# Attention and a spectral filter on one core: chunk order, later values, filter products on GpSimd

## The chip, the cores and the metric

The kernel runs on one core of one Trainium2 chip. The core has five engines with a queue of instructions each: TensorE (PE in the profile), VectorE (DVE), ScalarE (ACT), GpSimd (POOL) and SyncE (SP, which issues most DMAs). Matmul results go to PSUM, which has eight banks of 128 partitions by 512 float32 values; the other operands lie in SBUF. The metric is the time of one execution in microseconds, as the median of several runs.

## The reference

Two branches are mixed by a gate g per row. S is 2048, D is 448, there are 16 heads of 28, and all inputs are bfloat16. Branch b uses the same x as branch a.

```python
def reference(A_x, A_wqkv, A_wo, B_x, B_w_r, B_w_i, gate_w):
    def _A_ref(x, wqkv, wo):
        ...
        qkv = (lambda x, *d: x.transpose(*d))((x @ wqkv).reshape(B, S, 3, H, Dh), 2, 0, 3, 1, 4)
        ...
        scores = jnp.einsum("bhqd,bhkd->bhqk", q, k) * scale
        p = _softmax(scores, axis=-1)
        o = jnp.einsum("bhqk,bhkd->bhqd", p, v)
        return (lambda x, *d: x.transpose(*d))(o, 0, 2, 1, 3).reshape(B, S, D) @ wo
    def _B_ref(x, w_r, w_i):
        X = (lambda x, axes=(-2,-1): jnp.fft.rfft2(x.astype(jnp.float32), axes=axes))(x, axes=(-2, -1))
        W = w_r + 1j * w_i
        X = X * W
        y = (lambda x, s, axes=(-2,-1): jnp.fft.irfft2(x, s=s, axes=axes).astype(jnp.bfloat16))(X, (S, D), axes=(-2, -1))
        return y
    x = A_x
    g = _sigmoid((x * gate_w).sum(-1, keepdims=True))
    a = _A_ref(x, A_wqkv, A_wo)
    b = _B_ref(x, B_w_r, B_w_i)
    return g * a + (1 - g) * b
```

## The kernel before

**Attention.** The 16 heads form four groups G of four. A chunk is one group with 512 queries (j from 0 to 3), so there are 16 chunks; before, they run in the order ci = 4 G + j. A chunk has 16 packs, one for each 128 keys (kt), and a pack has four units, one per head: a score matmul with 32 rows of contraction into one PSUM bank, the exponential, and a product with the values that adds into the bank psV. Keys and queries of a group lie in KT[G % 2] and QT[G % 2], so those of group G can be projected when group G - 2 has no scores left.

**Two ways to the exponential.** A pack of kind A goes through ScalarE: two score tiles of two banks each (psA, psB) and one activation per tile into the ring P of 20 slots (L862; the first packs into VS). A pack of kind D goes through VectorE: its four scores go to single banks psX, an add and a maximum turn each into the bits of a bfloat16 (L891), and three shifted copies are made of the whole pack (L897); all four sets are multiplied with the values and add up, which stands for the exponential. Which pack is of which kind is settled when the program is built.

**The other work.** It is cut into units that borrow a psX bank: the transposes of x, the projections of K, Q (L1116) and values (v, L1276), the first transform of the filter (f1), then for each of 16 slices g: f2, f3, the product with the complex filter W, and i1; then i2 for 16 t's, and the 16 output tiles (L1474). In a slice, f3 leaves its result in PSUM, VectorE multiplies it twice (by the real and by the imaginary part, L1384), GpSimd adds and subtracts (L1391), and i1 on PE reads the sums. After each chunk VectorE copies psV to osb (L1449), the row sums go through DRAM (rs, rgd, RB: four, one and four DMAs on SP), and GpSimd multiplies osb by RB (L1458) into ON. An output tile is one matmul group with the filter's result Z and three with ON (groups 0 to 2), and then one with ON of group 3. The last chunk is normalised by transposes on VectorE (L1468 to L1472). Output tiles leave through four slots of ost, and a slot is free when its store has landed.

**What sets the order.** A planner (class Plan) runs when the program is built. It walks through the work with a duration per operation, gives each engine its next operation by priority, due time and free banks, and writes out one fixed order per engine; nothing is rearranged on the chip. Units have a point (at, in chunks of progress) from which they may start, and a due point. Operations of VectorE and GpSimd that are marked port are not laid on top of each other in the plan. When PE's load over a window is below z_hard, a group of matmuls with zero weights is put in. Score tiles in this text are counted in PE's order: there are 400 of them, one for each activation of L862.

Of the kernel before, what the change touches and what calls it, by code (L numbers as in the profile page):

```python
# [20 lines left out]
C = 112  # L21
# [6 lines left out]
BITS_MIN = 256.0  # L28

# [128 lines left out]
class Plan:  # L158
# [3 lines left out]
    def __init__(self, cfg):  # L162
        self.cfg = cfg
        self.out = []
# [108 lines left out]
    def run(self):  # L273
# [18 lines left out]
        limit = 1200.0  # L292
        while self.npend > 0 or not self.stream_over():
            eng = min(self.T, key=self.T.get)
            t = self.T[eng]
            if t > limit:
# [113 lines left out]
    def next_tile(self):  # L410
# [7 lines left out]
        while len(units) < size:  # L418
            if cur is None:
# [31 lines left out]
        self.tile = dict(k=k, units=units, ready=ready, slots=slots, grp=k % len(self.sizes))  # L451
        self.ntile += 1
        return self.tile

# [38 lines left out]
    def exp_run(self, e, t):  # L493
# [11 lines left out]
        for p, h in e["units"]:  # L505
            a = self.act_pack[p]
            a["exps"].append(o)
            if len(a["exps"]) == 4:
                ci, kt = divmod(p, 16)
                x = Op("PE", 0, None, [self.v_ready[ci // 4][kt]] + a["exps"], name="pv")  # L510
# [47 lines left out]
    def d_run(self, d, h, bank, t, conc):  # L558
# [19 lines left out]
        self.s_mark(d["p"] // 64, o.end)  # L578
# [3 lines left out]
    def d_sums(self, d):  # L582
        p = d["p"]
        ci, kt = divmod(p, 16)
        vr = self.v_ready[ci // 4][kt]
# [34 lines left out]
    def pe_step(self, t):  # L620
# [35 lines left out]
        pool = c["xbanks"] if (self.started or self.reserve) and any(self.s_left) else self.allb  # L656
# [67 lines left out]
    def s_run(self, tl, t):  # L724
# [13 lines left out]
        for p, h in tl["units"]:  # L738
            G = p // 64
# [5 lines left out]
        fb = self.free_banks(t, self.cfg["xbanks"])  # L745
# [82 lines left out]
    tiles=(2, 2), xbanks=("X0", "X1", "X2"), nring=20, nvar=10, nearly=5, l_pe=0.09, l_act=0.03, pe_lat=0.20,  # L828
    dma_issue=0.6, m_pe=0.2, m_bank=0.1, tol=0.15, max_ahead=9, nd_max=99, d_open=3, ahead=3, d_chunks=1,
    dve_op1=0.605, dve_shift=0.60, pool_shift=2.0, pool_shifts=(), pool_every=0, prio_op1=3, prio_shift=3, sh_max=4, d_urg=0,  # L830
    window=3.413, z_hard=3250, z_soft=3500,
    w_pv=1.0, w_open=0.5, w_new=1.6, w_late=0.5, w_d=3, w_due=2, hungry=1.4, v_rush=0.5, x_rush=4.0, k_rush=5.0, q_rush=0.0, w_hungry=1, sw_pen=0, pv_min=1, ring_urg=2, d_first=True,
# [3 lines left out]
class Emit:  # L836
# [5 lines left out]
    def score(self, p, h, bank):  # L842
        k = self.k
        ci, kt = divmod(p, 16)
        G, j = divmod(ci, 4)
# [27 lines left out]
    def value(self, p, h, rhs, x):  # L873
        k = self.k
        ci, kt = divmod(p, 16)
        G = ci // 4
# [27 lines left out]
class Kernel:  # L904
# [27 lines left out]
    def tiles(self, ctx):  # L932
# [9 lines left out]
        self.psX = [ps.tile([128, 512], F32, name=f"psX{i}") for i in range(len(CFG["xbanks"]))]  # L942
# [37 lines left out]
        self.Wo = sb("Wo", [128, NG, D])  # L980
# [4 lines left out]
        self.t12 = [[sb(f"t{n}{i}", [128, 2 * FP]) for n in (1, 2)] for i in range(2)]  # L985
        self.P = sb("P", [128, CFG["nring"], 512])
# [25 lines left out]
    def plan(self):  # L1012
# [5 lines left out]
        for i, b in enumerate(CFG["xbanks"]):  # L1018
            pl.banks[b] = self.psX[i][:, :]
# [40 lines left out]
    def loads(self):  # L1060
# [10 lines left out]
        self.d_wv = self.dma(self.Wv[0:C, :, 0:D], w3[:, :, 2 * D:3 * D], 9.4, **fast)  # L1071
        self.d_gw = self.dma(self.Wv[0:C, :, D:D + 1], self.gw.rearrange("(c k o) -> k c o", c=NC, o=1), 9.4)
# [21 lines left out]
        self.m_wo = pl.op("POOL", 1.9, lambda e: nc.gpsimd.memset(self.Wo[:, :, :], 0.0), prio=6, port=True)  # L1094
        self.d_wo = []
        wov = self.wo.rearrange("(g h d) n -> h d g n", g=NG, h=4)
        for h in range(4):
            self.d_wo.append(self.dma(self.Wo[32 * h + 1:32 * h + 29, :, :], wov[h], 3.0, [self.m_wo, self.d_bi], prio=7))
# [31 lines left out]
    def square(self, eng, src, i, deps, prio=4, alt=None):  # L1130
# [9 lines left out]
    def head(self):  # L1140
        pl, nc = self.pl, self.nc
        self.o_xT = [[] for _ in range(4)]
        for b in range(4):
            for cp in range(2):
                u = pl.unit(-10, "xT", due=-1, rush=6.0 if b == 0 else CFG["x_rush"])
# [24 lines left out]
        u = pl.unit(-8, "w", due=-1, rush=6.0)  # L1170
# [10 lines left out]
        self.m_wo.deps.append(self.o_wt)  # L1181
        self.queries(0, -6.9945, None, [1, 2, 3], "DVE", deps=[self.o_wt])

    def first(self, which, b, name, sel, one):
# [3 lines left out]
        u = self.proj((-9.5 if b == 0 else -9.0) + 0.1 * b, which, 0, b, name, due=-1, rush=6.0 if b == 0 else CFG["k_rush"])  # L1188
# [13 lines left out]
    def queries(self, G, at, nk, blocks, eng, deps=(), alt=None, span=0.0):  # L1202
# [3 lines left out]
        due = at + 1.5 if G else 0.3  # L1206
# [38 lines left out]
    def group(self, G, at, span=0.18):  # L1245
# [3 lines left out]
        for b in range(4):  # L1249
            u = self.proj(at + span * b, 0, G, b, "k", deps=free, due=at + 1.2)  # L1250
            self.k_ready[G][b] = self.ev_k(u, G, b, deps=free)
            sqs.append(self.square("POOL", self.KT[G % 2][:, 512 * b:512 * b + 512], b, [self.k_ready[G][b], self.sq_use[b]]))
        u = pl.unit(at + span * 4, "kn", due=at + 1.3)
# [12 lines left out]
        u = pl.unit(at + span * 4, "kb", due=at + 1.3)  # L1266
        u.mm(lambda bank: self.mm(bank[:, 0:1], self.mrow4[:, :, :].rearrange("p b h -> p (b h)"), self.one[0:1, 1:2], True, True), n=60, kind="row", deps=[b2])
        nk = u.use("DVE", 0.1, lambda bank, e: nc.vector.tensor_copy(out=self.nks[G % 2][:, :], in_=bank[:, 0:1]), prio=2)
        self.queries(G, at + span * 5, nk, [0, 1, 2, 3], "POOL", deps=free, span=span)


    def values(self):
        nc = self.nc
        self.o_g, evs = [], []
        for t in range(NT):
# [6 lines left out]
            def ev(bank, e, t=t):  # L1282
                out = self.Vb[:, t, :, 1:29]
                in_ = bank[:, 0:448].rearrange("p (h d) -> p h d", d=DH)
                nc.scalar.copy(out=out, in_=in_) if e == "ACT" else nc.vector.tensor_copy(out=out, in_=in_)
            o = u.use("DVE", dict(DVE=0.54, ACT=0.5), ev, deps=[self.m_v1], alt="ACT", prio=2)
            evs.append(o)
            for G in range(1, NG):
                self.v_ready[G][t] = o
            self.o_g.append(u.use("DVE", 0.09, lambda bank, e, t=t: nc.vector.tensor_copy(out=self.glog[:, t:t + 1], in_=bank[:, 448:449]), prio=2))  # L1290
        for b in range(4):
# [4 lines left out]
            o = self.pl.op("DVE", dict(DVE=0.54, POOL=1.0), weigh, evs[4 * b:4 * b + 4] + [self.o_wt], prio=0, port=True)  # L1296
            for t in range(4 * b, 4 * b + 4):
                self.v_ready[0][t] = o

    def gate(self):  # L1300
        pl, nc = self.pl, self.nc
        a = pl.op("ACT", 0.12, lambda e: nc.scalar.activation(out=self.ge[:, :], in_=self.glog[:, :], func=ACT.Exp, scale=-1.0), self.o_g)
        a = pl.op("DVE", 0.1, lambda e: nc.vector.tensor_scalar_add(out=self.ge[:, :], in0=self.ge[:, :], scalar1=1.0), [a], port=True)
        a = pl.op("DVE", 0.25, lambda e: nc.vector.reciprocal(out=self.ge[:, :], in_=self.ge[:, :]), [a])
# [239 lines left out]
```

## Time and profile before

The median of three runs is 417.62 us (414.58 to 419.14). The profiled execution took 417.98 us, of which the span from the first to the last instruction is 416.2 us; its granted TensorE clock is 0.992.

| engine | work in the span | instructions |
|---|---|---|
| PE | matmuls, 394.5 us busy | 5030 |
| DVE | bits, shifts, evictions, 367.7 us | 677 |
| ACT | exponentials above all, 382.4 us | 418 |
| POOL | squares, sums, normalising products, 102.4 us | 144 |

The page divides the span into 40 slices and gives the busy share of each engine in tenths. A line of the groups gives the source line, the engine and operation, output and inputs with shapes, the count, the busy time, the mean duration of one, and the idle time of the engine just before them with what ended it. Durations of instructions that overlap add up to more than the engine's busy time, so the interval from start to start is taken from the timeline. The line number of a matmul is that of a helper (L913), so matmuls are told apart by their tiles.

### The profile page before, as it was taken

The page shows a single profiled execution, that of the slowest core. Times are in us where ns is not written, and L with a number is a line of the kernel's source. Part 1 is how long each engine was busy: PE and PEld are TensorE (multiplying, and loading weights), DVE is VectorE, ACT ScalarE, POOL GpSimd, SP SyncE. Part 2 cuts the span into 40 slices and gives each one's busy share as a digit, 9 for nine tenths or more (in the row PEclk, how much of TensorE's full clock was granted, in tenths as well). Part 3 has the DMA queues.
Part 4 walks back from the last instruction along what each step waited for, and adds up shares of the span by engine and source line. Part 5 has one row for each costly group of instructions (what it writes and reads, how often), then busy time and mean ns, then how long its engine had stood idle before and what let it go on. Part 6 is the DMA issues. An engine that isn't in the chain of part 4 may idle for free.

```text
span 416.2 us, 12278 instructions
## 1 busy us (share of the span) xinstructions
PE 394.5 (95%) x5030; PEld 136.2 (33%) x5030; DVE 367.7 (88%) x677; ACT 382.4 (92%) x418; POOL 102.4 (25%) x144
## 2 busy tenths in 40 slices
PE   7999999999999999999999999999999999999993
PEld 4433343222333323323333223223333322223251
DVE  3547699999999999989999899899998999999991
ACT  3895989999999999999999999999999989999941
POOL 0251102652221323331302242251367111010100
PEclk9999999999999999999999999999999989999998
DMA  8520001221022202021121201100100100010203
GB/s 263 151 62 7 4 2 17 53 41 39 11 57 52 84 8 63 4 64 32 37 74 46 58 8 59 39 28 4 28 3 2 28 2 27 4 50 4 70 8 106
DMA packets 23929, 17.66 MB, mean 42 GB/s; under 512 B 15268, under 2 KB 19281, under 8 KB 23873
## 3 DMA queue, kind: packets, MB, share of 16 engines
q1 hardware_dynamic: 22800, 16.59, 14.8%
q8 instruction: 39, 0.64, 0.7%
q10 hardware_dynamic: 1072, 0.29, 0.3%
q14 instruction: 18, 0.14, 0.1%
HBM read 14.71 MB, written 1.97 MB: 40 GB/s over the span
## 4 chain that ended last, share of the span: by engine, by line
PE 42%; ACT 25%; DVE 16%; issue 6%; DMA 6%; SPq 2%; ACTq 0%; DVEq 0%; POOL 0%
ACT P L862 25%; PE psX L913 15%; PE psV L913 13%; PE psB L913 7%; PE psA L913 7%; DVE VS L897 5%; DVE VS L891 5%; DMA rs<-osb 3%; DMA Qf<-in_A_wqkv_dram 2%; SPq L1055 2%; DMA out_dram<-ost 2%; DVE osb L1449 1%; DVE t L1384 1%; DVE tab L1426 1%; DVE QT L1220 0%
## 5 line engine op out<-in xcount | busy, mean ns | idle before, releaser
L862 ACT ACTIVATE P<-psA 128x1024 bf16<-128x1024 f32 x195 | 205.9, 1056 | 7.7 <-PE psV L913 5.4
L862 ACT ACTIVATE P<-psB 128x1024 bf16<-128x1024 f32 x195 | 206.0, 1056 | 3.3 <-PE psB L913 2.1
L891 DVE TENSOR_SCALAR VS<-psX 128x512 int16<-128x512 f32 x224 | 145.4, 680 | 6.1 <-PE psX L913 5.5
L897 DVE TENSOR_SCALAR VS<-VS 128x2048 int16<-128x2048 int16 x168 | 111.1, 714 | 0.4
L913 PEld LDWEIGHTS <-KT 32*128 32x128 bf16 (+1 forms) x1040 | 46.0, 91 | 144.4 <-issue 141.4
L913 PE MATMUL psV<-VS,Vb 128*32 128x512 bf16 x916 | 82.2, 389 | 2.0 <-DVE VS L897 1.7
L913 PE MATMUL psB<-QT,KT 32*128 32x512 bf16 x400 | 78.4, 384 | 5.9 <-ACT P L862 5.0
L913 PE MATMUL psA<-QT,KT 32*128 32x512 bf16 x400 | 79.7, 384 | 1.1 <-ACT P L862 0.6
L913 PE MATMUL psV<-P,Vb 128*32 128x512 bf16 x780 | 74.6, 386 | 0.0
L913 PE MATMUL psX<-QT,KT 32*128 32x512 bf16 x224 | 73.1, 384 | 1.3 <-DVE VS L891 0.6
L913 PEld LDWEIGHTS <-Vb 128*32 128x32 bf16 x1696 | 36.7, 94 | 64.8 <-issue 59.1
L1391 POOL TENSOR_TENSOR t<-t,t 128x226 bf16<-128x226 bf16 x32 | 19.1, 618 | 59.2 <-DVE t L1384 49.9
L1137 POOL TENSOR_TENSOR sq<-QT 128x512 bf16<-128x512 bf16 x16 | 17.1, 1071 | 59.9 <-DVE QT L1220 33.5
L1458 POOL TENSOR_TENSOR xtok<-osb,RB 128x512 bf16<-128x512 f32 x12 | 15.8, 1318 | 39.8 <-DMA RB<-rgd 39.8
L1432 POOL TENSOR_TENSOR UZ<-tab 128x225 bf16<-128x225 f32 (+1 forms) x32 | 19.4, 632 | 17.8 <-DMA RB<-rgd 9.5
L1137 POOL TENSOR_TENSOR sq<-KT 128x512 bf16<-128x512 bf16 x12 | 12.9, 1072 | 39.5 <-DVE KT L1127 38.8
L913 PE MATMUL psX<-xT,Wq 112*32 112x512 bf16 x240 | 19.6, 383 | 0.2 <-DVE VS L891 0.2
L913 PE MATMUL psX<-xT,Wk 112*32 112x512 bf16 x240 | 19.8, 384 | 0.0
L913 PE MATMUL psX<-Bd,UZ 112*32 112x452 bf16 x256 | 19.1, 358 | 0.0
L1384 DVE TENSOR_TENSOR t<-psX,Wf 128x452 bf16<-128x452 f32 x32 | 18.9, 617 | 0.0
L1458 POOL TENSOR_TENSOR xT<-osb,RB 128x512 bf16<-128x512 f32 x3 | 4.4, 1454 | 56.2 <-DMA RB<-rgd 56.2
L913 PE MATMUL psX<-Wv,xT 112*32 112x449 bf16 x240 | 16.0, 357 | 0.0
(111 smaller groups left out, 307.0 us busy)
## 6 DMA issues: line engine op xcount, KB each, us to landing
tab<-c_tab SPq DMA_DIRECT2D x16, 256.0 KB
RB<-rgd SPq DMA_DIRECT2D x60, 64.0 KB
xtok<-in_A_x_dram SPq DMA_DIRECT2D x4, 448.0 KB
out_dram<-ost SPq DMA_DIRECT2D x6, 224.0 KB
rs<-osb SPq DMA_DIRECT2D x60, 2.0 KB
Wf<-in_B_w_r_dram SPq DMA_DIRECT2D x31, 28.1 KB
Wf<-in_B_w_i_dram SPq DMA_DIRECT2D x31, 28.1 KB
Qf<-in_A_wqkv_dram SPq DMA_DIRECT2D x2, 294.0 KB
```

The source lines that it names most:

```text
L862: k.nc.scalar.activation(out=out, in_=k.psS[e["grp"]][:, 0:n, :], func=ACT.Exp, scale=LN2_128)
L891: k.nc.vector.tensor_scalar(out=k.VS[:, slot, 512 * h:512 * h + 512], in0=bank, scalar1=float(BITS0), scalar2=BITS_MIN, op0=ALU.add, op1=A ...
L897: k.nc.vector.tensor_scalar(out=k.VS[:, dst, :], in0=k.VS[:, src, :], scalar1=float(SHIFTS[v - 1]), scalar2=None, op0=ALU.add)
L913: self.nc.tensor.matmul(out, lhsT=lhsT, rhs=rhs, start=start, stop=stop, skip_group_check=True, **kw)
L1055: (self.nc.sync if e == "SP" else self.nc.scalar).dma_start(out=out, in_=in_)
L1137: (self.nc.vector if e == "DVE" else self.nc.gpsimd).tensor_tensor(out=sq[:, :], in0=src, in1=src, op=ALU.mult)
L1384: ts.append(u.use("DVE", 0.55, lambda bank, e, i=i, q=q: nc.vector.tensor_tensor(out=self.t12[i][q][:, :].rearrange("p (r f) -> p r f", r= ...
L1391: (nc.vector if e == "DVE" else nc.gpsimd).tensor_tensor(out=t1[:, FP * q:FP * q + FP], in0=t1[:, FP * q:FP * q + FP], in1=t2[:, FP - FP * ...
L1426: c = u.use("DVE", 0.54, lambda bank, e, eo=eo: nc.vector.tensor_copy(out=eo, in_=bank[:, 0:450]), deps=self.i1_last + use[t % 2])
L1432: nc.gpsimd.tensor_tensor(out=z, in0=a, in1=b, op=ALU.subtract if q else ALU.add)
L1449: ev = pl.op("DVE", 0.61, lambda e: nc.vector.tensor_copy(out=self.osb[:, :], in_=self.psV[:, :]), [pl.pv_done[ci], prev], prio=0, name="e ...
L1458: prev = pl.op("POOL", 1.3, lambda e, G=G, j=j: nc.gpsimd.tensor_tensor(out=self.ON[G][:, 512 * j:512 * j + 512], in0=self.osb[:, :], in1= ...
```

## The change

**Chunk order.** A table CHUNKS replaces ci = 4 G + j: groups 0 and 1 as before, then (2,0) (2,1) (3,0) (3,1) (2,2) (3,2) (2,3) (3,3). Everything that took G and j from the chunk's number reads the table. The points and due points of the group projections change (group 3 from 8.3 to 8.0, with its eight projections 0.06 instead of 0.18 apart).

**Values.** The 16 units of 449 columns (448 values and the gate) become four units (four t's each) of 113 columns, group 0's values and the gate column, and 16 units v2 of 336 columns, for groups 1 to 3, which may start from 2.0 chunks of progress on. The load of the value weights is cut in two accordingly.

**Filter products.** VectorE copies f3's result to a new float32 buffer FX, and GpSimd makes the two products from there.

**Score banks.** The bank of a unit comes from a list in the score tile, a tile may be cut short at the end of the ring or of the first packs, and the number of psX banks follows from the tile sizes. The sizes stay (2, 2).

**Output.** The 16 output tiles get earlier points for j below 3; the last four are cast into the sq tiles instead of ost. The normalising of the last chunk is ordered by t. Wo lies in the space of Bd, so its clearing and its four loads come after the last f2.

**Planner settings.** Many weights change, and some of them differ by chunk of progress. In the orders that come out, ScalarE has 402 activations (201 packs) instead of 400, and VectorE 220 and 165 operations of the kinds L891 and L897 instead of 224 and 168 (55 packs instead of 56). PE has 5258 matmuls instead of 5030.

```diff
+CHUNKS = [(0, j) for j in range(4)] + [(1, j) for j in range(4)] + [(2, 0), (2, 1), (3, 0), (3, 1), (2, 2), (3, 2), (2, 3), (3, 3)]
...
-        a, b = self.q_ready[ci], self.k_ready[ci // 4][kt // 4]
+        G, j = CHUNKS[ci]
+        a, b = self.q_ready[4 * G + j], self.k_ready[G][kt // 4]
...
+            if units and self.apart(units, cur, na, taken):
+                break
...
+    def apart(self, units, cur, na, taken):
...
+        if units[0][0] < c["nearly"]:
+            return p >= c["nearly"]
+        return (self.nunit + len(units)) % c["nring"] == 0
...
-            self.score(p, h, self.k.pl.bank_ap(f"{'AB'[tl['grp']]}{i}"))
+            self.score(p, h, self.k.pl.bank_ap(tl["banks"][i]))
...
-        self.Wo = sb("Wo", [128, NG, D])
+        self.Wo = self.Bd[:, :, :].rearrange("p c f -> p (c f)")[:, 0:NG * D].rearrange("p (g d) -> p g d", g=NG)
...
+        self.FX = [sb(f"FX{i}", [128, 2 * FP], F32) for i in range(2)]
...
-        self.group(1, 1.0)
+        self.group(1, CFG["g_at"][0], due=CFG["g_due"])
...
-        self.group(2, 4.3)
-        self.group(3, 8.3)
+        self.group(2, CFG["g_at"][1], due=CFG["g_due"])
+        self.group(3, CFG["g_at"][2], 0.06, 0.4)
...
-        self.d_wv = self.dma(self.Wv[0:C, :, 0:D], w3[:, :, 2 * D:3 * D], 9.4, **fast)
-        self.d_gw = self.dma(self.Wv[0:C, :, D:D + 1], self.gw.rearrange("(c k o) -> k c o", c=NC, o=1), 9.4)
+        self.d_wv = self.dma(self.Wv[0:C, :, 0:112], w3[:, :, 2 * D:2 * D + 112], 9.4, **fast)
+        self.d_wv2 = self.dma(self.Wv[0:C, :, 113:449], w3[:, :, 2 * D + 112:3 * D], 9.4)
+        self.d_gw = self.dma(self.Wv[0:C, :, 112:113], self.gw.rearrange("(c k o) -> k c o", c=NC, o=1), 9.4)
...
+        for b in range(4):
+            u = self.pl.unit(-0.1 + 0.001 * b, "v", due=0.1 + b / 4, rush=CFG["v_rush"])
+            for k in range(4):
+                def go(bank, t=4 * b + k, k=k):
+                    for c in range(NC):
+                        self.mmc(bank[:, 113 * k:113 * k + 113], self.xT[0:C, c, 128 * t:128 * t + 128], self.Wv[0:C, c, 0:113], c == 0, c == NC - 1)
+                u.mm(go, n=113, count=4, kind="bg", eff=0.875, deps=self.o_xT[b] + [self.d_wv, self.d_gw])
...
         for t in range(NT):
-            u = self.pl.unit(-7 + 0.001 * t, "v", due=(t + 2) / 16, rush=CFG["v_rush"])
-            b = t // 4
+            u = self.pl.unit(CFG["v2_at"] + 0.11 * t, "v2", due=CFG["v2_due"] + 0.05 * t)
             for c in range(NC):
-                u.mm(lambda bank, c=c, t=t: self.mmc(bank[:, 0:449], self.xT[0:C, c, 128 * t:128 * t + 128], self.Wv[0:C, c, :], c == 0, c == NC - 1),
-                     n=449, kind="bg", eff=0.875, deps=self.o_xT[b] + [self.d_wv, self.d_gw])
...
+                u.mm(lambda bank, c=c, t=t: self.mmc(bank[:, 0:336], self.xT[0:C, c, 128 * t:128 * t + 128], self.Wv[0:C, c, 113:449], c == 0, c == NC - 1),
+                     n=336, kind="bg", eff=0.875, deps=self.o_xT[t // 4] + [self.d_wv2])
...
+            fx = u.use("DVE", 0.55, lambda bank, e, i=i: nc.vector.tensor_copy(out=self.FX[i][:, :], in_=bank[:, 0:452]), deps=fuse[i])
             ts = []
             for q in range(2):
-                ts.append(u.use("DVE", 0.55, lambda bank, e, i=i, q=q: nc.vector.tensor_tensor(
-                    out=self.t12[i][q][:, :].rearrange("p (r f) -> p r f", r=2), in0=bank[:, 0:452].rearrange("p (r f) -> p r f", r=2),
-                    in1=self.Wf[i][:, q:q + 1, :].to_broadcast([128, 2, FP]), op=ALU.mult), deps=loads[g][1:] + tuse[i]))
+                ts.append(pl.op("POOL", 1.2, lambda e, i=i, q=q: nc.gpsimd.tensor_tensor(
+                    out=self.t12[i][q][:, :].rearrange("p (r f) -> p r f", r=2), in0=self.FX[i][:, :].rearrange("p (r f) -> p r f", r=2),
+                    in1=self.Wf[i][:, q:q + 1, :].to_broadcast([128, 2, FP]), op=ALU.mult), [fx] + loads[g][1:] + tuse[i], port=True, prio=2))
...
+        self.m_wo = pl.op("POOL", 1.9, lambda e: nc.gpsimd.memset(self.Wo[:, :, :], 0.0), [self.f2_last], prio=6, port=True)
...
-            u = pl.unit(13.0 + j + 0.25 * (t % 4) - (0.6 if j == 3 else 0.0) if j < 3 else 16.5, "out")
+            at = (12.6, 13.2, 14.3, 15.99)[j] + (0.15 if j < 3 else 0.001) * (t % 4)
+            u = pl.unit(at, "out", due=at + 0.5 if j < 3 else 99.0)
...
-                out = self.ost[:, t % 4, :]
+                out = self.ost[:, t % 4, :] if t < 12 else self.sq[t % 4][:, 0:D]
...
-            evs.append(u.use(eng, dict(DVE=0.54, ACT=0.5), ev, deps=[dm[t // 2 - 2]] if t >= 4 else []))
+            evs.append(u.use(eng, dict(DVE=0.54, ACT=0.5), ev, deps=[dm[t // 2 - 2]] if 4 <= t < 12 else []))
```

More of the change, by code (lines that the diff above doesn't have):

```diff
@@ L163, in __init__ @@
         self.cfg = cfg
+        self.xbanks = [f"X{i}" for i in range(7 - sum(cfg["tiles"]))]
+        self.cfgs = [dict(cfg, **cfg["seg"].get(i, {})) for i in range(18)]
         self.out = []
@@ L941, in tiles @@
         self.psS = [ps.tile([128, n, 512], F32, name=f"ps{'AB'[i]}") for i, n in enumerate(sizes)]
-        self.psX = [ps.tile([128, 512], F32, name=f"psX{i}") for i in range(len(CFG["xbanks"]))]
+        self.psX = [ps.tile([128, 512], F32, name=f"psX{i}") for i in range(7 - sum(sizes))]
         self.psV = ps.tile([128, 512], F32, name="psV")
@@ L1017, in plan @@
                 pl.banks[f"{'AB'[i]}{k}"] = self.psS[i][:, k, :]
-        for i, b in enumerate(CFG["xbanks"]):
-            pl.banks[b] = self.psX[i][:, :]
+        for i, x in enumerate(self.psX):
+            pl.banks[f"X{i}"] = x[:, :]
         pl.allb = list(pl.banks)
@@ L1295, in weigh @@
                                                                      in1=v[:, :, :, 0:1].to_broadcast([128, 4, 4, DH]), op=ALU.mult)
-            o = self.pl.op("DVE", dict(DVE=0.54, POOL=1.0), weigh, evs[4 * b:4 * b + 4] + [self.o_wt], prio=0, port=True)
+            o = self.pl.op("DVE", dict(DVE=0.54, POOL=1.0), weigh, [evs[b], self.o_wt], prio=0, port=True)
             for t in range(4 * b, 4 * b + 4):
                 self.v_ready[0][t] = o
+            for x in [self.o_w[G, i] for G in range(1, NG) for i in range(2)]:
+                x.deps.append(o)
@@ L1306, in gate @@
-        a = pl.op("DVE", 0.1, lambda e: nc.vector.tensor_scalar(out=self.gg[:, 1, :], in0=self.gg[:, 0, :], scalar1=-1.0, scalar2=1.0, op0=ALU.mult, op1=ALU.add), [a], port=True)
-        u = pl.unit(0.0, "gT", due=0.9)
+        a = pl.op("ACT", 0.12, lambda e: nc.scalar.activation(out=self.ge[:, :], in_=self.glog[:, :], func=ACT.Exp, scale=-1.0), self.o_g, prio=-1)
+        a = pl.op("DVE", 0.1, lambda e: nc.vector.tensor_scalar_add(out=self.ge[:, :], in0=self.ge[:, :], scalar1=1.0), [a], port=True, prio=1)
@@ L1310, in gate @@
-        d = self.dma(self.gd[:, :], self.grow[:, :], 2.1, [a])
+        a = u.use("DVE", 0.2, lambda bank, e: nc.vector.tensor_copy(out=self.grow[:, :], in_=bank.bitcast(BF16)[0:32, 0:128]), prio=1)
+        d = self.dma(self.gd[:, :], self.grow[:, :], 2.1, [a], prio=1)
         g = self.gd[:, :]
-        self.d_gq = [self.dma(self.gq[32 * h:32 * h + 32, :, :], raw_ap(g, [[16, 32], [512, 4], [1, 16]]), 2.3, [d]) for h in range(4)]
+        self.d_gq = [self.dma(self.gq[32 * h:32 * h + 32, :, :], raw_ap(g, [[16, 32], [512, 4], [1, 16]]), 2.3, [d], prio=1) for h in range(4)]
```

144 lines of the change are left out of this document (84 added, 60 removed).

## The prediction

> **What bounds the kernel now.** I read the page's busy shares and slices first, then the groups by line, then the timeline where a slice falls short, then the tail.
>
> ```profile
> PE 394.5 (95%) x5030; PEld 136.2 (33%) x5030; DVE 367.7 (88%) x677; ACT 382.4 (92%) x418; POOL 102.4 (25%) x144
> ...
> DVE  3547699999999999989999899899998999999991
> ACT  3895989999999999999999999999999989999941
> ```
>
> Three engines are full at once; GpSimd is a quarter full. ScalarE lacks work in slices 1 to 5 and in the last two (a slice is 10.4 us).
>
> ```profile
> L862 ACT ACTIVATE P<-psB 128x1024 bf16<-128x1024 f32 x195 | 206.0, 1056 | 3.3 <-PE psB L913 2.1 <-PE psX L913 0.9
> L891 DVE TENSOR_SCALAR VS<-psX 128x512 int16<-128x512 f32 x224 | 145.4, 680 | 6.1 <-PE psX L913 5.5
> L897 DVE TENSOR_SCALAR VS<-VS 128x2048 int16<-128x2048 int16 x168 | 111.1, 714 | 0.4
> L1384 DVE TENSOR_TENSOR t<-psX,Wf 128x452 bf16<-128x452 f32 x32 | 18.9, 617 | 0.0
> L1137 POOL TENSOR_TENSOR sq<-KT 128x512 bf16<-128x512 bf16 x12 | 12.9, 1072 | 39.5 <-DVE KT L1127 38.8
> L1458 POOL TENSOR_TENSOR xtok<-osb,RB 128x512 bf16<-128x512 f32 x12 | 15.8, 1318 | 39.8 <-DMA RB<-rgd 39.8
> ```
>
> ScalarE's 400 exponentials overlap: they last 1.056 us, but in the timeline full stretches start one every 0.905 us. The first starts at 17.39 us, the last at 399.25, so 399 intervals take 381.9 where 361.1 would do. By stage: numbers 1 to 40 take 43.5 us (floor 36.2, and 1.1 for two small activations between them), 41 to 280 take 224.5 (floor 217.2), 281 to 400 take 113.9 (floor 107.7). After the last come 15.9 us of tail. So a gain has two large homes: stage 1 and the tail.
>
> Stage 1 has one hole:
>
> ```profile
> 35.55 1.14 ACT L862 ACTIVATE P<-psB 128x1024 bf16<-128x1024 f32 x1
> 37.18 2.86 PE L913 MATMUL psX<-Wv,xT 112*32 112x449 bf16 x56
> 40.98 1.02 ACT L862 ACTIVATE P<-psA 128x1024 bf16<-128x1024 f32 x1 [4.29 <-PE psV L913]
> ```
>
> The ring for exponentials is full. It is emptied by products with values, which need values, and PE is still projecting those. Start to start this costs 5.43 - 0.91 = 4.5 us.
>
> The tail:
>
> ```profile
> 399.25 1.02 ACT L862 ACTIVATE P<-psB 128x1024 bf16<-128x1024 f32 x1
> 401.15 0.91 DVE L1468 STREAM_TRANSPOSE osb<-psV 128x128 f32<-128x128 f32 x4 [0.57 <-PE psV L913]
> 403.31 0.88 DVE L1472 STREAM_TRANSPOSE xT<-brow 128x128 bf16<-128x128 bf16 x4
> 409.31 1.16 DVE L1490 CAST ost<-psB 128x448 bf16<-128x448 f32 x2 [3.54 <-DMA out_dram<-ost]
> 413.00 0.54 ACT L1490 CAST ost<-psB 128x448 bf16<-128x448 f32 x1
> ```
>
> Normalising ends at 404.2; then nine output tiles are still to be evicted through four slots of ost, each waiting for a store.
>
> **The change part by part.**
>
> *Values.* PE ran 64 groups (four matmuls side by side) of 449 columns, (2.86 - 0.17) / 14 = 0.192 us each: 12.3 us, all before score tile 32. Now 64 groups of 113 columns stay there, and 64 of 336 go to score tiles 75 to 121. The latter cost 0.192 x 336/449 = 0.144: 9.2 us. No row shows 113 columns: 0.047 by columns, 0.10 as the 225-column groups on Bi (sixteen matmuls in 0.57 us); I take 0.07, so 4.5 us, with 3.0 and 6.4 as ends. Net +1.4 (-0.1 to +3.3), but 7.8 leave stage 1. DVE: sixteen evictions at 0.60 with the gate column become four at 0.60 and sixteen at about 0.41: -0.6. One DMA more.
>
> *Filter.* DVE drops 32 products at 0.54 start to start (17.3 us) and gains 16 copies of the same size (8.6): -8.7. GpSimd gains 32 products of 452 elements, one operand f32. The rows on both sides are sq (bf16, 1.04 undisturbed) and xtok (f32, 1.27): scaled by 452/512, 0.92 to 1.12; I take 1.05, so 33.6 us, which takes GpSimd from 102 to 136. The cover: in the new order PE's i1 stands 6 to 18 score tiles behind its f3, 5.5 us at least, and the path is 0.5 + 0.65 + 2 x 1.05 + 2 x 0.55 = 4.4. If the cover goes, PE waits in order at i1, with the next score tile and so ScalarE behind it. On GpSimd's queue the products also stand behind the normalising product that waits for RB (39.8 us over 12); in the new order it falls between the two products of one g twice, with i1 eight tiles or more away.
>
> *Split.* ScalarE takes 201 of 256 packs instead of 200, DVE 55 instead of 56: +2 x 0.905 = +1.8 on ScalarE, -(4 x 0.60 + 3 x 0.63) = -4.3 on DVE. DVE sheds 13.6 us in all.
>
> *Score banks.* The tiles are still two pairs of banks, and no tile is split: nothing.
>
> *Alternating chunks.* Group 3 is first needed at score tile 261, not 307; its last row (brow) now stands at tiles 245 to 249, 12 tiles or 11 us ahead. The rows' DMAs need about 4 us, by RB, which was issued at 390.20 and used at 393.67. So 7 us are spare. In return twelve output tiles stand inside the stream, the last four alone behind it, and those are cast into sq, which no store holds.
>
> *Output weights.* Wo moves into Bd: the clearing (1.6 us on GpSimd) and four loads (1.65 us of SP) move from 26 us to behind the last f2, score tile 262; first use is tile 336. Nothing.
>
> **The sum,** against the profiled execution (416.2 span, 417.98 whole). Adding group costs (score tile 0.22, 0.10 for each change of matmul shape, 0.217 for 512 columns) over PE's two orders gives stage 1: 42.8 before, which 43.5 measured bears out, and 36.4 after; stage 2: 210.2 and 215.1.
> - Before the first exponential: same instructions, transposes earlier: 17.4 (+-0.7).
> - Stage 1: PE no longer leads, so ScalarE's 37.3 + 0.6 = 37.9 (37.3 to 40).
> - Stage 2: six of twelve blocks of 20 tiles now hold over 18.0 us of PE work. Before, two such blocks (18.2, 18.1) took 18.5 and 18.9, the usual one 18.4. So six at 18.45 and six at PE work plus 0.45: 223.6 (219 to 229).
> - Stage 3: 113.9 and two exponentials: 115.8. PE has room there (16 to 17 per 18.1); DVE's relief lies mostly earlier. Ends: 112 (121 x 0.92), and 119 with 3 us of DVE work not hidden.
> - Tail: last exponential 1.0, then 0.6 to the transposes (0.9 before, where shifted values came last), 3.3 for DVE's chain (3.05 before, now interleaved), 0.4 last matmuls, 0.55 cast, 2.7 from the end of the last cast to the end of the span (413.5 to 416.2): 7.6 (7 to 11).
> 17.4 + 37.9 + 223.6 + 115.8 + 1.0 + 7.6 = 403.3 of span, 12.9 less; 417.98 - 12.9 = 405.1. The profiled execution is 0.36 above the median, so 404.8.
>
> **What speaks against it: GpSimd and DVE in each other's way.**
>
> ```profile
> 275.57 3.33 DVE L897 TENSOR_SCALAR VS<-VS 128x2048 int16<-128x2048 int16 x3
> 275.73 0.94 POOL L1391 TENSOR_TENSOR t<-t,t 128x226 bf16<-128x226 bf16 x1 [0.63 <-DVE t L1384]
> 276.67 1.68 POOL L1458 TENSOR_TENSOR xtok<-osb,RB 128x512 bf16<-128x512 f32 x1
> 398.69 1.89 DVE L897 TENSOR_SCALAR VS<-VS 128x2048 int16<-128x2048 int16 x3
> ```
>
> Three shifts alone take 1.89 us; amid GpSimd work 3.33, and GpSimd's rows stretch too (0.55 to 0.94, 1.27 to 1.68). Of 48 such triples 13 overlap GpSimd and six are slowed, 5.0 us together. GpSimd's busy time grows by a third, so I add 2 us to DVE, inside its 13.6. The Trainium skill, "SBUF — State Buffer", section "SBUF: two separate sides", states that VectorE in a two-port mode and GpSimd hold a shared port pair exclusively for a whole instruction and the loser blocks. By that rule the six slowed triples agree, and in the seven others DVE would have been the holder; it is the ground of the slower rival below.
>
> **The rivals.**
> - *PE becomes the bound* (0.15). Stage 2 carries 4.9 us more PE work. The 14.3 us between PE's work and the stage's length before would have to stay on top: 229.4, so 411. For: blocks of 18.5. Against: in stage 1 only 0.7 of 43.5 was such an addition.
> - *The last chunk's gate* (0.10). Chunk 14 is now group 2's last, and the last four output tiles need its normalised rows in their first matmuls, which stand ahead of the last products with values. Its eviction stands at score tile 384 of 402, about 15.3 us before the last exponential ends; the same chain before ran from 381.30 to 394.94, 13.6. Should it be late by 3 us, PE and the tail wait: 408.
> - *Slower: the shared access decides* (0.08). The filter runs over some 33 triples of shifts. If each were delayed like the worst (1.44), DVE loses 48 us; it has 10 spare (windows of 20 us from 60 to 280: 210.5 busy of 220) and sheds 13.6: 24 over, which makes 429. It costs from 0.7 us per triple upward and outweighs the gain from 1.1 (36.5 us over 33); before, the mean was 0.1.
> - *Given back later* (0.07). DVE's relief is early and stage 3 keeps its shifts and gains output evictions; at 0.99 us per exponential there, and PE's bound too, 415.
>
> **How the numbers follow.** The forecast has 0.60, range 401 to 409, time 405. To 413 it takes in PE's bound and the late gate: about 0.82 with those below 400 left out. Faster by over 1% (below 413.4; 1% is about what this measurement can tell from no change): 0.60 + 0.15 + 0.10 = 0.85. Within 1%: 0.07. Slower: 0.08.
>
> **What would show it.** The interval from exponential 1 to 40 near 38 us with no wait on psV; 402 exponentials; L897 triples still mostly 1.89; new GpSimd products of 0.9 to 1.15 us; PE not waiting on GpSimd at t; tail of 7 to 8 us with no wait on out_dram. Wrong if PE's waits on GpSimd or on DVE's shifts sum to over 6 us, or if stage 2 exceeds 229.

## The result and the profile after

The changed kernel takes 413.73 us (median of 20 runs, 411.86 to 420.08) and the kernel before 418.15 on the same chip. The ratio is 0.990 (0.988 to 0.993), a gain of 4.4 us where 12.9 were forecast. The time lies 4.7 us above the forecast's 401 to 409, and 0.7 above the 413 to which it reached with PE's bound and the late gate. The profiled execution took 411.96 us with a span of 410.2, 6.9 longer than the 403.3 of the sum. In some executions of nearly every kernel the granted TensorE clock drops for some tens of us; ratios leave the most disturbed ones out, and a stage time is read only where the clock was full, or with the clock beside it.

The page of the changed kernel, busy shares and slices:

```profile
PE 390.6 (95%) x5258; PEld 135.0 (33%) x5258; DVE 368.6 (90%) x647; ACT 385.7 (94%) x419; POOL 140.0 (34%) x176
...
DVE  3668999988888999899999879999999999999994
ACT  3799999999999999999999999998999999999993
```

ScalarE's hole in slices 1 to 5 is gone. DVE was to shed 13.6 us and is as busy as before (368.6 against 367.7). Its groups, and GpSimd's, say where the relief went:

```profile
L928 DVE TENSOR_SCALAR VS<-psX 128x512 int16<-128x512 f32 x220 | 144.0, 679 | 10.7 <-PE psX L950 9.6
L934 DVE TENSOR_SCALAR VS<-VS 128x2048 int16<-128x2048 int16 x165 | 122.4, 789 | 0.3
...
L1427 POOL TENSOR_TENSOR t<-FX,Wf 128x452 bf16<-128x452 f32 x32 | 34.1, 1083 | 49.0 <-DVE FX L1424 33.5
L1507 POOL TENSOR_TENSOR xtok<-osb,RB 128x512 bf16<-128x512 f32 x12 | 17.0, 1420 | 66.6 <-DMA RB<-rgd 63.9
```

There are three shifts fewer (L934), and together they take 11.3 us more (122.4 against 111.1). The casts from PSUM (L928) last what they did. From the start of one exponential to another, by the timeline, with the forecast:

| stage | before | forecast | after | after, with waits both ways (below) |
|---|---|---|---|---|
| start of the first exponential | 17.4 | 17.4 | 16.9 | 17.3 |
| 1 to 40 | 43.5 | 37.9 | 37.6 | 37.9 |
| 41 to 280 | 224.5 | 223.6 | 228.1 | 223.3 |
| 281 to the last | 113.9 (119 gaps; clock 0.83 from 335 to 345 us) | 115.8 (121) | 118.2 (121) | 113.4 (121) |
| last exponential and tail | 16.9 | 8.6 | 9.3 | 9.3 |

The head, stage 1 and the tail came out as forecast. The hole in stage 1, in the timeline after:

```profile
34.97 1.17 ACT L899 ACTIVATE P<-psB 128x1024 bf16<-128x1024 f32 x1
35.86 0.38 PE L950 MATMUL psX<-Wv,xT 112*32 112x113 bf16 x16
36.03 1.03 ACT L899 ACTIVATE P<-psA 128x1024 bf16<-128x1024 f32 x1
```

The values take PE 0.38 us at a time where they took 2.86, and the next exponential is 1.06 us away instead of 5.43. The tail:

```profile
400.86 1.03 ACT L899 ACTIVATE P<-psB 128x1024 bf16<-128x1024 f32 x1
...
402.93 0.51 DVE L1517 STREAM_TRANSPOSE osb<-psV 128x128 f32<-128x128 f32 x2 [1.28 <-PE psV L950]
...
405.36 1.40 ACT L1540 CAST sq<-psX 128x448 bf16<-128x448 f32 x3 [3.47 <-DVE brow L1520]
...
406.91 0.53 ACT L1540 CAST sq<-psB 128x448 bf16<-128x448 f32 x1
```

Four casts stand behind the chain, and none waits for a store. All that is missing lies in the two long stages, 4.5 and 2.4 us over the forecast, each still inside the ends given for it. There PE waits for DVE's shifts; these are PE's waits from 60 to 395 us, before and then after (engine, tile and line waited for; us, times, longest):

```profile
PE psB L913 <- ACT P L862: 5.0, 16, 0.5
PE psX L913 <- DVE VS L891: 2.0, 7, 0.5
PE psV L913 <- DVE VS L897: 1.7, 5, 0.6
```

```profile
PE psV L950 <- DVE VS L934: 6.4, 19, 0.7
PE psX L950 <- DVE VS L928: 1.9, 9, 0.2
PE psB L950 <- ACT P L899: 1.6, 6, 0.4
```

The first line after, 6.4 us, is over the 6 that the prediction named as a sign of being wrong.

And this is what a slow run of shifts looks like, in the timeline after (DVE's and GpSimd's lines):

```profile
256.83 0.68 DVE L928 TENSOR_SCALAR VS<-psX 128x512 int16<-128x512 f32 x1
257.40 1.54 POOL L1435 TENSOR_TENSOR t<-t,t 128x226 bf16<-128x226 bf16 x2
257.43 3.48 DVE L934 TENSOR_SCALAR VS<-VS 128x2048 int16<-128x2048 int16 x3
258.91 2.88 POOL L1427 TENSOR_TENSOR t<-FX,Wf 128x452 bf16<-128x452 f32 x2
260.84 1.28 DVE L928 TENSOR_SCALAR VS<-psX 128x512 int16<-128x512 f32 x2
```

Three shifts last 3.48 us instead of 1.89, two sums 1.54 instead of 1.10, two products 2.88 instead of 1.98. I call the time over 0.66, 1.29 and 1.89 us for one, two and three shifts in a row (and 0.62 more for each further one) their **excess**, summed from 40 us on. Before it was 5.2 us, with 14 of 62 such rows of shifts touched by GpSimd and six slowed; after it is 17.8, with 24 of 67 touched and 19 slowed. By stretches of time (40 to 170, 170 to 282, from 282 us) it is 4.4, 7.9 and 5.5. The expectations below give 20.6 for the changed kernel: that sum counts twice what belongs to rows of shifts that cross a multiple of 25 us.

### The profile page after: what moved, and what is told of

It reads as the page before. It is cut to its first block, busy times and chain, and to the rows that moved or that the text cites. A ratio compares the mean times of both kernels' runs of the same rounds, so it can differ in the third digit from the quotient of the medians.

```text
span 410.2 us, 12740 instructions
## 1 busy us (share of the span) xinstructions
PE 390.6 (95%) x5258; PEld 135.0 (33%) x5258; DVE 368.6 (90%) x647; ACT 385.7 (94%) x419; POOL 140.0 (34%) x176
## 4 chain that ended last, share of the span: by engine, by line
PE 52%; DVE 35%; ACT 4%; DMA 3%; issue 3%; SPq 1%; ACTq 0%; DVEq 0%
PE psX L950 19%; PE psV L950 15%; DVE VS L934 15%; DVE VS L928 13%; PE psB L950 9%; PE psA L950 9%; ACT P L899 4%; DMA rs<-osb 2%; DMA Qf<-in_A_wqkv_dram 1%; DVE tab L1475 1%; SPq L1093 1%; DVE ost L1540 1%; DVE FX L1424 1%; DVE osb L1498 1%; DVE P L1415 1%
## 5 line engine op out<-in xcount | busy, mean ns | idle before, releaser
L928 DVE TENSOR_SCALAR VS<-psX 128x512 int16<-128x512 f32 x220 | 144.0, 679 | 10.7 <-PE psX L950 9.6
L934 DVE TENSOR_SCALAR VS<-VS 128x2048 int16<-128x2048 int16 x165 | 122.4, 789 | 0.3
L950 PEld LDWEIGHTS <-KT 32*128 32x128 bf16 (+1 forms) x1040 | 43.8, 91 | 136.0 <-issue 133.1
L950 PE MATMUL psX<-QT,KT 32*128 32x512 bf16 x220 | 76.0, 383 | 1.9 <-DVE VS L928 1.2
L950 PE MATMUL psV<-P,Vb 128*32 128x512 bf16 x784 | 73.6, 385 | 0.3 <-DVE osb L1498 0.2
L1427 POOL TENSOR_TENSOR t<-FX,Wf 128x452 bf16<-128x452 f32 x32 | 34.1, 1083 | 49.0 <-DVE FX L1424 33.5
L1507 POOL TENSOR_TENSOR xtok<-osb,RB 128x512 bf16<-128x512 f32 x12 | 17.0, 1420 | 66.6 <-DMA RB<-rgd 63.9
L1435 POOL TENSOR_TENSOR t<-t,t 128x226 bf16<-128x226 bf16 x32 | 20.3, 654 | 1.2
L950 PE MATMUL psX<-Wv,xT 112*32 112x336 bf16 (+1 forms) x448 | 17.7, 268 | 0.0
L950 PEld LDWEIGHTS <-xT 112*32 112x32 bf16 (+1 forms) x576 | 10.7, 96 | 10.2 <-issue 6.8
```

The costliest lines, as they stand in the source:

```text
L928: k.nc.vector.tensor_scalar(out=k.VS[:, slot, 512 * h:512 * h + 512], in0=bank, scalar1=float(BITS0), scalar2=BITS_MIN, op0=ALU.add, op1=A ...
L934: k.nc.vector.tensor_scalar(out=k.VS[:, dst, :], in0=k.VS[:, src, :], scalar1=float(SHIFTS[v - 1]), scalar2=None, op0=ALU.add)
L950: self.nc.tensor.matmul(out, lhsT=lhsT, rhs=rhs, start=start, stop=stop, skip_group_check=True, **kw)
L1427: ts.append(pl.op("POOL", 1.2, lambda e, i=i, q=q: nc.gpsimd.tensor_tensor(out=self.t12[i][q][:, :].rearrange("p (r f) -> p r f", r=2), in ...
L1435: (nc.vector if e == "DVE" else nc.gpsimd).tensor_tensor(out=t1[:, FP * q:FP * q + FP], in0=t1[:, FP * q:FP * q + FP], in1=t2[:, FP - FP * ...
L1507: prev = pl.op("POOL", 1.3, lambda e, G=G, j=j: nc.gpsimd.tensor_tensor(out=self.ON[G][:, 512 * j:512 * j + 512], in0=self.osb[:, :], in1= ...
```

## The experiments

Theory A: GpSimd's operations slow the shifts, DVE loses in this way what the filter gave it, and that is the whole miss. Stage 2 is the one from exponential 41 to 280, stage 3 the one from 281 on. Rivals: PE's added work bounds stage 2 (B), and DVE's work or the output tiles inside the stream bound stage 3 (C).

### Less work for GpSimd

First the products alone, on 2 of 452 columns, so that the filter is not computed:

```diff
-   out=self.t12[i][q][:, :]..., in0=self.FX[i][:, :]..., in1=self.Wf[i][:, q:q + 1, :]...
+   out=self.t12[i][q][:, 0:2], in0=self.FX[i][:, 0:2], in1=self.Wf[i][:, q, 0:2]
```

> The changed kernel with its instruction order kept on every engine; the 32 filter products on GpSimd work on 2 of 452 columns (the filter's result is left out), and the products' buffers are cleared once at the start. Theory A (shared access: GpSimd's new products delay the shifts on VectorE, PE waits in order for shifted copies, ScalarE starves): what the runs of shifts take beyond 0.63 us each falls from 20.6 us to 6 to 10, the interval from exponential 41 to 281 falls from 228.1 to 223 to 225, and the time falls by 4 to 8 us, to 406 to 410. Rival B (PE is the bound: its matmuls are the same here): 413 to 415, stage 2 at 228. Rival C (the planner's new order holds too much VectorE work behind tile 280): stage 2 falls a little, exponentials 281 to 402 stay at 118, 411 to 413.

Measured: 409.5 us, ratio 0.980 (0.972 to 0.989). Stage 2 fell to 224.6, with the same matmuls in the same order, so B falls. Stage 3, which has no products, stayed at 118.2, as A and C both allow. The excess fell to 11.2, short of the 6 to 10 expected. Then the 32 combinations of stage 3 as well:

```diff
-   nc.gpsimd.tensor_tensor(out=z, in0=a, in1=b, ...)
+   nc.gpsimd.tensor_tensor(out=z[:, 0:2], in0=a[:, 0:2], in1=b[:, 0:2], ...)
```

> As e1_small_products, and the 32 sums and differences of the last transform on GpSimd work on 2 columns as well (the filter's branch is left out of the output). Theory A: on top of the first, the exponentials 281 to 402 fall from 118.2 us to 114 to 116 (the excess of the shifts there was 6.5 us); 404 to 408. Rival B: 413 to 415. Rival C: exponentials 281 to 402 stay at 117 or more.

Measured: 417.28 us, where 404 to 408 were expected. The clearing that this needs ran on DVE and delayed the first exponential to 20.5 us, and the clock was 0.80 from 17 to 60 us. Stage 3, at a full clock, took 115.6 us, so C falls. The clearing was then moved to GpSimd:

```diff
+   for p in self.t12:
+       for t in p:
+           self.nc.gpsimd.memset(t[:, :], 0.0)
+   self.nc.gpsimd.memset(self.UZ[96:128, 0:NT * D], 0.0)
```

> The changed kernel with the 32 GpSimd products on 2 of 452 columns and the 32 combining operations of stage 3 on 2 of 225 columns; nothing else moves on PE, DVE or ScalarE, and the buffers that are now written only in part are cleared on GpSimd at the very start. Theory (GpSimd's operations slow DVE's shifts, in stage 2 by the products and in stage 3 by the combinations): stage 1 stays near 37.6, stage 2 falls from 228.1 to 224-225.5, stage 3 from 118.2 to 115-116.5, the head and the tail stay, and the time is 405 to 408 us. Rival (PE's own work bounds stage 2 and the twelve output tiles inside the stream bound stage 3): stage 2 stays above 227, stage 3 above 117.5, and the time is 411 or more.

Measured: 409.5 us, 0.978 (0.973 to 0.984), where 405 to 408 were expected; a miss in the sum, since head and stage 1 took 3.0 us more than in the changed kernel (first exponential at 18.2, stage 1 39.3 with a clock of 0.96 from 17 to 55 us). The two long stages fell as theory A has it, stage 2 to 224.2 and stage 3 to 116.6 (0.1 above the range given). The excess was still 9.2 us: squares, sums and normalising products were left.

### The filter's place

Products on DVE again, in the changed kernel (planned anew, 406 exponentials):

```diff
-   fx = u.use("DVE", 0.55, lambda bank, e, i=i: nc.vector.tensor_copy(out=self.FX[i][:, :], in_=bank[:, 0:452]), ...)
-   ts.append(pl.op("POOL", 1.2, lambda e, i=i, q=q: nc.gpsimd.tensor_tensor(
+   ts.append(u.use("DVE", 0.55, lambda bank, e, i=i, q=q: nc.vector.tensor_tensor(
```

> The changed kernel with the filter products back on VectorE, straight from PSUM; the planner then gives ScalarE 406 activations and VectorE 53 packs. Theory A: the excess of the shifts falls to 4 to 8 us, VectorE does 8.7 us more of products but 8.5 us less of packs, ScalarE 3.6 us more; 411 to 415, so that the move to GpSimd gave nothing. Rival B: PE's work is the same, 413 to 415. If the move to GpSimd was a gain after all: 416 to 420.

Measured: 415.96 us, 0.997 (0.994 to 1.001), between the two forecasts. The excess is 10.3 us, above the 4 to 8 expected, although GpSimd is no busier than in the kernel before (102.3 us against 102.4, with 5.2 of excess), so the order of the work alone can make the two meet more. Head and stage 1 are as in the changed kernel (17.3 and 37.7), so their gain does not come from the filter. In stage 3 the clock fell, to 0.60 from 340 to 350 us, which clouds the rest. So the same with more filler on PE:

```diff
-        10: dict(ring_urg=10, hungry=0, z_hard=3550, sh_max=1),
+        10: dict(ring_urg=10, hungry=0, z_hard=3700, sh_max=1),
...
```

> Products back on DVE as in the run before of that kind, and more filler matmuls in chunks 6 to 14, so that PE has no slack window (the filler threshold goes from 3450-3550 to 3700); 404 exponentials. If the low granted clock at 330 to 350 us was what made stage 3 of that run 125.5 us, the clock stays at 1.00, stage 3 falls to 118-120 (two more gaps than the changed kernel), and the time is 409 to 412 us: the filter's way to GpSimd then bought nothing. If the clock was not the cause, stage 3 stays above 123 and the time is 415 or more.

Measured: 419.24 us as the median of ten; the five at a clock of 0.996 or more took 414.1 to 416.2, and the ratio is 0.991 (0.987 to 0.995). The forecast was missed: the clock costs something in the run before this, but with the clock full the products on DVE are still no better than 414. Their ratio cannot be told from the changed kernel's 0.990; by the executions at a clock of 0.996 or more the changed kernel, in its own runs, is 2.6 us ahead (medians 412.9 and 415.6). So without more, the filter's way to GpSimd buys 0.7% at most. The other corner, the kernel before with the products on GpSimd and one FX:

```diff
+   self.FX = [sb("FX0", [128, 2 * FP], F32)] * 2
...
+   fx = u.use("DVE", 0.55, lambda bank, e, i=i: nc.vector.tensor_copy(out=self.FX[i][:, :], in_=bank[:, 0:452]), ...)
-   ts.append(u.use("DVE", 0.55, lambda bank, e, i=i, q=q: nc.vector.tensor_tensor(
+   ts.append(pl.op("POOL", 1.2, lambda e, i=i, q=q: nc.gpsimd.tensor_tensor(
```

> The kernel before with the filter products alone moved to GpSimd (one buffer FX for lack of space). Theory A: the excess of the shifts rises from 5 to 12 to 18 us and takes back the 8.7 us of VectorE; 417 to 420, no gain over the kernel before. If VectorE's relief were free, as the prediction had it (2 us of contention): 412 to 415.

Measured: 423.13 us, 1.014 (1.006 to 1.021), above the 417 to 420 expected. The excess rose from 5.2 to 10.0, less than expected, so the loss is not the excess alone. The clock fell to 0.50 in stage 3 of the profiled execution, but two others, at 0.997 and 0.998, still took 421.9 and 421.5 us. With one FX each copy waits for the products ahead of it; whether that costs the rest was not tested.

A narrower copy:

```diff
-   self.FX = [sb(f"FX{i}", [128, 2 * FP], F32) for i in range(2)]
+   self.FX = [sb(f"FX{i}", [128, 2 * FP]) for i in range(2)]
```

> The changed kernel with the copy FX in bf16 instead of f32, the plan unchanged. If GpSimd's time for a product follows the width of its input, a product falls from 1.08 to about 0.92 us (the bf16 squares scaled by 452/512), 5 us less of GpSimd work, and the slowed shifts of stage 2 lose about a sixth of their 14 us: 411 to 413 us. If the copy's width does not matter to GpSimd, the product stays at 1.08 and the time at 413 to 414.

Measured: 413.97 us, 0.990 (0.983 to 0.996), and a median product of 0.998 us against 1.014. The width of the copy hardly matters to GpSimd.

### The order of the chunks

```diff
-   ... (2, 0), (2, 1), (3, 0), (3, 1), (2, 2), (3, 2), (2, 3), (3, 3)]
+   ... (2, 0), (2, 1), (2, 2), (2, 3), (3, 0), (3, 1), (3, 2), (3, 3)]
```

> The changed kernel with the chunks of groups 2 and 3 in their old order (406 exponentials in the new plan). If alternation is what put the output tiles inside the stream, eight casts stand behind the last exponential instead of four and the tail is 11 to 14 us instead of 8.3; stage 3 has four more gaps (+3.6) and less of its output work, so 117 to 122; in all 414 to 419 us. If the tail's gain came from the casts into sq alone, the tail stays below 9.5 us.

Measured: 417.76 us, 0.999 (0.996 to 1.003). The tail behind the last exponential is 10.6 us against 8.3: eight casts follow the last exponential instead of four. That is under the 11 to 14 expected but over 9.5, so alternation and the casts into sq share the tail's gain. The ratio gives back nearly all of the 4 us, but that cannot be put down to the order: no execution had a clock above 0.992, where the changed kernel's were mostly at 0.994 or more. In the profiled one the clock was 0.80 from 17 to 60 us and 0.50 from 275 to 285. Its stage 3, at a full clock, took 116.9 us for 125 intervals, less for each than the changed kernel's. What is shown of the old order is the 2.3 us of the tail.

### The same work, kept apart

The last test changes no work and no order. In the changed kernel each marked GpSimd operation waits for the DVE shift (or small marked operation) that the plan puts ahead of it; in the second run, which alone has the three lines with pool, the shifts (and the small marked operations of DVE) also wait for GpSimd:

```diff
+   if eng == "DVE" and o.port:
+       shift = last
+       if pool is not None:
+           self.tc.add_manual_dep(last, pool.name, dep, reason="port")
+   elif eng == "POOL" and o.port and shift is not None:
+       self.tc.add_manual_dep(last, shift.name, dep, reason="port")
+       pool = last
```

> The changed kernel, full work and the same order on every engine; each of GpSimd's operations on shared memory (products, sums, squares, combinations, normalising products) also waits for the DVE shift that the plan puts ahead of it. Theory (the time is lost where a GpSimd operation falls on a shift): GpSimd's work moves behind the triples into the casts from PSUM, which it does not slow; the excess of the shifts falls from 20.6 to 10-14 us, stage 2 to 225-227, stage 3 to 116-117.5, the time to 409-412 us. If GpSimd is then late for PE (waits of PE on t or sq over 3 us), the time stays at 413-415. Rival (the plan already keeps them apart as far as it can, and the overlaps come from shifts that start behind a GpSimd operation): excess stays at 18 or more, time 413-414.

> As the run with waiting products, and each DVE shift also waits for the GpSimd operation that the plan puts ahead of it, so that no two of them meet at all. The shifts then last 0.63 us each (excess under 3 us), but DVE stands still where GpSimd is late, with casts queued behind. If those standstills are less than the 20.6 us of excess that they replace, 407-411 us; if GpSimd's lateness (its waits for DMA, for example 50 to 65 us in all for RB) reaches DVE, 418 us or more.

Measured: 402.99 us, 0.963 (0.956 to 0.970), and 402.66 us, 0.965 (0.960 to 0.971). Both gain far more than expected, and both beat both kernels. The excess is 3.0 and 0.7 us. The same stretch of the filter with waits both ways, in the timeline:

```profile
254.79 0.68 DVE L928 TENSOR_SCALAR VS<-psX 128x512 int16<-128x512 f32 x1
255.39 1.89 DVE L934 TENSOR_SCALAR VS<-VS 128x2048 int16<-128x2048 int16 x3
257.19 1.28 DVE L928 TENSOR_SCALAR VS<-psX 128x512 int16<-128x512 f32 x2
257.42 1.10 POOL L1444 TENSOR_TENSOR t<-t,t 128x226 bf16<-128x226 bf16 x2 [2.08 <-DVE VS L934]
258.39 0.62 DVE L1424 CAST P<-psX 128x452 bf16<-128x452 f32 x1
258.48 1.99 POOL L1436 TENSOR_TENSOR t<-FX,Wf 128x452 bf16<-128x452 f32 x2
```

The sums wait 2.08 us for the shifts and then run beside casts from PSUM, which they do not slow. Its page, busy shares and the chain of work that ended last, its group of shifts, and PE's wait for them from 60 to 395 us:

```profile
PE 386.2 (96%) x5258; PEld 133.1 (33%) x5258; DVE 352.4 (88%) x647; ACT 382.7 (95%) x419; POOL 127.3 (32%) x176
...
PE 58%; DVE 17%; ACT 16%; issue 4%; DMA 3%; SPq 1%; POOL 1%; ACTq 0%; DVEq 0%
...
L934 DVE TENSOR_SCALAR VS<-VS 128x2048 int16<-128x2048 int16 x165 | 105.3, 689 | 3.2 <-POOL R1s L1369 1.2
...
PE psV L950 <- DVE VS L934: 2.1, 5, 0.9
```

The same 165 shifts are busy for 105.3 us instead of 122.4, 17.1 less, and PE waits 2.1 us for them instead of 6.4. GpSimd gains too: 127.3 us busy instead of 140.0. DVE is 16.2 us less busy and its share of the chain falls from 35% in the changed kernel to 17%; the shifts stood only 3.2 us idle, so the fear that GpSimd's lateness would reach DVE was wrong. Last, the same waits in the kernel before and with the products on DVE:

> The kernel before with the same waits in both directions between GpSimd's operations and DVE's shifts, nothing else changed. Before had 5.1 us of excess on its shifts against 20.6 after, and its losses lay in stage 1 (the hole at 36 to 41 us) and in the tail, which the waits do not touch. If the waits are worth what the excess is, the time falls by 1 to 4 us, to 414-417. If they are worth as much here as in the changed kernel (11 us), the excess is the wrong measure and 407-409 follows.

> The changed kernel with the products on DVE (its own plan, 406 exponentials) and the same waits in both directions. The excess there was 10.4 us. If moving the filter to GpSimd is worth something once nothing overlaps, this stays 3 us or more above the 402.7 of the changed kernel with both waits: 406-412. If the filter's place is indifferent, 402-404.

Measured: 413.96 us, 0.985 (0.977 to 0.993), and 410.46 us, 0.980 (0.971 to 0.990); just under the 414 to 417 and inside the 406 to 412 expected; the excess is under 0.4 us in both. Together, as ratios to the kernel before on the same chip:

| | without waits | waits both ways |
|---|---|---|
| kernel before | 1 | 0.985 |
| changed, products on DVE | 0.997 (0.991 with filler) | 0.980 |
| changed, products on GpSimd | 0.990 | 0.965 |

With nothing meeting, moving the filter is worth 0.965 / 0.980, 1.5% or 6 us, and the whole change 0.965 / 0.985, 2.0% or 8 us. The intervals leave about 1% either way, and the run with the products on DVE has a plan of its own. By the executions at a clock of 0.99 or more (402.4 to 403.0, 409.9 to 410.9 and 412.7 to 414.4 us) it is about 7 and 11 us. Without waits these are 0.7% at most (0.990 / 0.997) and 1.0%.

## Why the prediction was wrong

**The step that failed** is the contention term: "GpSimd's busy time grows by a third, so I add 2 us to DVE, inside its 13.6." The mechanism was named, with its rows; its size was not 2 us but 12.6 (5.2 to 17.8). Two things in it were wrong.

*Scaled by busy time.* GpSimd's busy time did grow by 37%. Its overlap with shifts, added up over the rows of shifts, grew from 15.4 to 35.5 us, and each us of it cost 0.50 of excess instead of 0.34. Only part of this is the filter's: with the products cut to 2 columns in the same order the excess is 11.2 us, and with the products on DVE, where GpSimd is no busier than before, 10.3. So of the 12.6 us some 7 come with the products and some 5 or 6 with the new order, to which the term gave nothing. The filter now has GpSimd work through products and sums in a row behind a copy by DVE: unbroken stretches of over 3 us, which span a whole triple, went from 5 to 15. That such stretches raise the cost of each us is my reading; no run tests it by itself. The plan does not lay these operations on each other, but it is made with 1.2 us for a product and 0.60 for a shift, where 1.01 and 0.63 were measured, and nothing on the chip held it to that until the waits did.

The rule cited, in the Trainium skill, "SBUF — State Buffer", section "SBUF: two separate sides", has the pair of ports held for a whole instruction by whichever of the two comes first. By that rule the trace agrees: no shift loses more than one GpSimd operation takes. The longest single shift after is 1.77 us, 1.1 more than one alone, beside a normalising product, which takes 1.27 alone; beside the filter's products, 1.01 alone, the longest is 1.50. The casts from PSUM last 0.680 us beside GpSimd work and 0.678 without.

*Taken as free inside the relief.* The rival priced the loss only beyond 10 us spare and 13.6 shed. But a shift can stand on the path at that moment. The chain of work that ended last, after, at the triple shown above:

```profile
256.29 0.63 DVE FX L1424
256.92 0.60 DVE VS L928
257.51 3.40 DVE VS L934 x3
260.92 0.61 DVE VS L928
261.53 0.04 issue
261.57 0.37 PE psX L950
```

The next cast stands in DVE's queue behind the slow shifts, and PE needs the bank that it empties. Waits both ways took 17.1 us of excess away and 9.0 us off the span, 0.53 us for each. The sum gave the 12.6 us of growth no time at all, and 12.6 x 0.53 = 6.7 of its 6.9 us miss. The 0.53 is the price in this pair of runs alone.

**The other steps.** Stage 1 (37.9, measured 37.6) and the tail (7.6, measured 8.3) were right for the reason given. Stage 2 by PE's work, 223.6, is what remains when nothing meets (223.3), in part by luck: its blocks of 18.45 us came from a stage that held some 3 us of excess itself. Stage 3 was forecast 115.8 from the 113.9 before, which held 2.0 us of excess and 10 us at a clock of 0.83. It was 118.2, 0.977 us per exponential. With waits both ways and a full clock it is 113.4 (0.937), and in the kernel before 110.5 (0.929). So a relief of DVE by the change does not show in stage 3; what the meetings cost there does. The products lasted 1.01 us alone (1.05 forecast). Output weights cost nothing that PE's waits show.

**The rivals.** PE as the bound gave 411, near the profiled 412.0, by luck: the same matmuls ran stage 2 in 224.6 and 223.3. The last chunk's gate did not show. "Given back later" gave 415, nearest to the median of 413.7, by luck too: it had one of the two places (stage 3 at 0.977 us per exponential, 0.99 forecast), but not the cause. Shared access was the cause at a quarter of its price: 12.6 us over the 33 triples it counted is 0.38 each, against 1.44, and under the 0.7 from which it was to cost anything.

**Left open.** Why the waits gain 1.5% in the kernel before (0.7 to 2.3%), whose excess was only 5.2 us. The clock may have a part: at 0.994 or more it took 412.7 to 414.0 us with the waits, and the kernel before took 414.7 to 418.4 without. Open too is what a rule for the clock would be.

## What to carry to other kernels

Moving work to an idle engine is not free if the two share something: price it by where the operations meet, not by busy time, and do not set the loss against relief elsewhere. When a plan keeps two kinds of operations apart in its own clock, only a wait keeps them apart on the chip. Here such a wait, with no change of work, was worth more than the whole change (402.7 us against 413.7).

## What was not expected of the hardware

The clock falls in the middle of a kernel with a busy PE. These are stretches of the kernel before with products on GpSimd (stretch, length, busy time and count of PE, PEld, DVE, ACT and POOL, granted clock, DMA share, GB/s):

```profile
330.00:340.00 10.00, 9.03 (x88) 2.77 (x87) 9.60 (x16) 9.92 (x11) 4.14 (x6) 0.96 0.00 0
340.00:350.00 10.00, 9.98 (x70) 2.00 (x70) 7.82 (x15) 7.35 (x8) 0.00 (x0) 0.50 0.03 3
350.00:360.00 10.00, 10.00 (x86) 2.32 (x74) 8.81 (x14) 8.01 (x9) 1.27 (x1) 0.69 0.11 28
```

PE was 90% busy ahead of the drop to 0.50; the changed kernel had stretches of 8.46 and 8.76 of 10 us at a clock of 1.00. So the busy share of 10 us does not tell when it falls. GpSimd's product takes the same time from a float32 as from a bfloat16 copy (1.01 and 1.00 us).
